# Reordering the first stage of a fused adaLN, linear-attention and GeGLU kernel: an earlier modulation quarter, two loads issued from ACT, and the eighth K tile ahead of the last wk rows

## The chip, the cores and the metric

The kernel runs on one core of a Trainium2 chip. The metric is the device time of one execution in microseconds (us), and a kernel's number is the median of its runs. Engines, as these traces have them: PE does matmuls (PEld is its weight load), DVE and ACT do elementwise work, POOL small things, SP issues DMAs.

## The reference, cut to what matters

```python
mod = (silu(c) @ w_mod).reshape(1, 6, 1, -1)          # w_mod: 1024 x 6144
sa, ca, ga, sb, cb, gb = (mod[:, i] for i in range(6))
h = layernorm(x) * (1 + ca) + sa                      # x: 1 x 2048 x 1024
x = x + ga * linear_attention(h, wqkv, wo)            # 32 heads; divides by pq . z
h = layernorm(x) * (1 + cb) + sb
x = x + gb * ((gelu(h @ w_gate) * (h @ w_up)) @ w_down)   # 3584 wide
```

Linear attention needs K and V of all tokens before any output, and each output is divided by a denominator per token and head. The first K matmul needs tokens, their layer norm, one quarter of the modulation (w_mod is loaded in quarters, because K's contraction goes over 8 rows of weights, two to a quarter) and two rows of wk.

## The kernel before

A helper records each operation in its engine's program, with its semaphores; in the trace PE's instructions start in the order of its program (from 7.03 us: transposes, seven fillers at 7.49, transposes at 9.28, one filler at 9.74, modulation at 9.95, six fillers at 10.76). PE's first stage in the kernel before (V = DVE, A = ACT, Q = SP in the code; `warm` are filler matmuls on zeros, `k_part(q, cs)` the K matmuls of weight rows 2q and 2q+1 for token tiles `cs`, `mod_cols(q)` the matmuls of modulation quarter q, `mod1` applies it on DVE, `t1` transposes on PE). K of the first four token tiles comes in two halves each, which makes eight K tiles. Seven of them are summed up side by side by `k_part`, each in its own bank of PSUM; the eighth, `kv_mm(3, "k", 1, 4, ...)`, has bank 4:

```python
sch.dma(Q, lambda e: e.dma_start(C8[:], c_v), ...)          # c, first of SP's DMAs
...
x_dma(0, 1); x_dma(1, 2); wmq_dma(0, (1,)); x_dma(2, 3)     # all from SP
wmq_dma(0, (0,)); x_dma(3, 4)
...                                                         # wk rows 2q, 2q+1 after quarter q
warm(12, 7)
...
t1(1, 6); warm(1, 7); mod_cols(0, 4, False); warm(6, 7)
...                                                         # tiles 2 and 3, quarters 1 to 3
k_part(2, [3])
warm(2)
k_part(3, [0, 1, 2, 3])                                     # 7 PSUM banks, rows 6 and 7
for (c_, jg), b in kb0.items():
    k_evac(c_, jg, b)                                       # ACT exp, DVE min, DVE add
kv_mm(3, "k", 1, 4, list(range(NDC)))                       # eighth K tile, bank 4
k_evac(3, 1, 4)
for c_ in range(4):
    for jg in range(2):
        b = nb()                                            # V in banks 0, 1, 2, 3 in turn
        kv_mm(c_, "v", jg, b, list(range(NDC)))
        v_evac(c_, jg, b)
```

## Time and profile before

| | before |
|---|---|
| median of the first runs | 847.55 us (845.94 to 847.57, 3 runs) |
| span of the profiled run (which took 846.43 us), mean PE clock | 844.6 us, 1.000 |
| first V matmul | 31.97 us |
| PE waits between 205 and 250 us | 0.89 and 1.26 us |

From PE's timeline of the first stage (start, duration, engine, line, operation, output<-inputs, count; in brackets the idle time before it and what ended that). L519 are transposes, L565 the modulation, L612 K and V, L668 fillers.

```profile
12.05 0.61 PE L519 MATMUL ps_all<-ident,xh 128*128 128x128 bf16 x8
...
19.75 0.54 PE L565 MATMUL ps_all<-siluT,wmq 128*128 128x1 bf16 x16
21.48 0.55 PE L565 MATMUL ps_all<-siluT,wmq 128*128 128x1 bf16 x16 [1.19 <-DMA wmq<-in_w_mod_dram]
...
25.56 0.94 PE L565 MATMUL ps_all<-siluT,wmq 128*128 128x1 bf16 x32
...
26.79 0.59 PE L668 MATMUL ps_all<-warm 128*128 128x512 bf16 x2
27.22 4.91 PE L612 MATMUL ps_all<-wk,h1T 128*128 128x512 bf16 x22
31.97 2.35 PE L612 MATMUL ps_all<-wv,h1T 128*128 128x512 bf16 x10
```

The third transposes start at 12.05, PE waits 1.19 us for a quarter of w_mod at 21.48, and K ends without a break in V at 31.97.

```profile
231.89 2.50 DVE L879 TENSOR_TENSOR pq<-pq,rb 128x512 bf16<-128x512 bf16 x4 [2.35 <-DMA rb<-scr_rd]
...
236.78 2.50 DVE L879 TENSOR_TENSOR pq<-pq,rb 128x512 bf16<-128x512 bf16 x4 [1.25 <-DMA rb<-scr_rd]
```

DVE waits for the broadcasts (2.35 and 1.25 us), PE for DVE (0.89 and 1.26 us). These two waits are the only ones of over 0.7 us between the start of V and the last matmul.

### The profile page before, as it was taken

The page shows a single profiled execution, that of the slowest core. Times are in us where ns is not written, and L with a number is a line of the kernel's source. Part 1 is how long each engine was busy: PE and PEld are TensorE (multiplying, and loading weights), DVE is VectorE, ACT ScalarE, POOL GpSimd, SP SyncE. Part 2 cuts the span into 40 slices and gives each one's busy share as a digit, 9 for nine tenths or more (in the row PEclk, how much of TensorE's full clock was granted, in tenths as well). Part 3 has the DMA queues.
Part 4 walks back from the last instruction along what each step waited for, and adds up shares of the span by engine and source line. Part 5 has one row for each costly group of instructions (what it writes and reads, how often), then busy time and mean ns, then how long its engine had stood idle before and what let it go on. Part 6 is the DMA issues. An engine that isn't in the chain of part 4 may idle for free.

```text
span 844.6 us, 11333 instructions
## 1 busy us (share of the span) xinstructions
PE 835.1 (99%) x4229; PEld 386.9 (46%) x4229; DVE 491.8 (58%) x883; ACT 294.9 (35%) x483; POOL 24.3 (3%) x64
## 2 busy tenths in 40 slices
PE   8999999999989999999999999999999999999998
PEld 4454444444434444444444444444444444444445
DVE  5676767877775555564456665445556635565522
ACT  2343333345504345520344442034544204444300
POOL 2000000000200000010000001000000000000000
PEclk9999999999999999999999999999999999999999
DMA  9991824029957587341455533055553305555000
GB/s 283 355 284 26 262 53 98 14 59 238 197 119 222 157 264 205 100 107 31 126 156 154 156 107 81 26 155 151 150 150 100 75 19 156 151 153 145 7 19 26
DMA packets 181750, 112.70 MB, mean 133 GB/s; under 512 B 33080, under 2 KB 172728, under 8 KB 180672
## 3 DMA queue, kind: packets, MB, share of 16 engines
q1 hardware_dynamic: 181696, 111.98, 48.6%
q8 instruction: 34, 0.56, 0.3%
q14 instruction: 20, 0.16, 0.1%
HBM read 100.67 MB, written 4.47 MB: 124 GB/s over the span
## 4 chain that ended last, share of the span: by engine, by line
PE 92%; DMA 4%; SPq 2%; DVE 1%; issue 0%; ACT 0%; DVEq 0%; ACTq 0%
PE ps_all L1025 23%; PE ps_all L1000 23%; PE ps_all L997 23%; PE ps_all L612 12%; PE ps_all L653 6%; PE ps_all L928 3%; DMA rb<-scr_rd 1%; DMA wmq<-in_w_mod_dram 1%; DMA h2T<-xh 1%; PE ps_all L634 1%; DVE pq L879 1%; DMA scr_rd<-rdc 1%; SPq L443 0%; SPq L438 0%; PE ps_all L584 0%; SPq L868 0%
## 5 line engine op out<-in xcount | busy, mean ns | idle before, releaser
L997 PE MATMUL ps_all<-h2T,wg 128*128 128x512 bf16 x896 | 339.6, 379 | 0.0
L1000 PE MATMUL ps_all<-h2T,wu 128*128 128x512 bf16 x896 | 339.6, 379 | 0.0
L1025 PE MATMUL ps_all<-wd,yT 128*128 128x512 bf16 (+1 forms) x924 | 194.1, 373 | 0.0
L1008 ACT ACTIVATE q<-ps_all 128x512 f32<-128x512 f32 x112 | 66.9, 597 | 233.9 <-PE ps_all L997 233.9
L1025 PEld LDWEIGHTS ps_all<-wd,yT 128*128 128x128 bf16 x924 | 90.4, 98 | 103.3
L1000 PEld LDWEIGHTS ps_all<-h2T,wu 128*128 128x128 bf16 x896 | 87.7, 98 | 105.7
L997 PEld LDWEIGHTS ps_all<-h2T,wg 128*128 128x128 bf16 x896 | 87.7, 98 | 105.7
L1010 DVE SCALAR_TENSOR_TENSOR ww<-q,ps_all 128x512 f32<-128x512 f32 x112 | 77.0, 687 | 92.5 <-ACT guh L1009 92.5
L1013 DVE SCALAR_TENSOR_TENSOR ww<-th,guh 128x512 f32<-128x512 f32 x112 | 77.5, 692 | 77.9 <-ACT th L1012 77.9
L1012 ACT ACTIVATE th<-ww 128x512 f32<-128x512 f32 x112 | 70.5, 629 | 84.3 <-DVE ww L1010 84.3
L1015 DVE TENSOR_TENSOR yT<-ww,ps_all 128x512 bf16<-128x512 f32 x112 | 76.9, 687 | 3.8
L1030 DVE TENSOR_TENSOR ps_all<-ps_all,gbb 128x512 f32<-128x512 f32 (+1 forms) x33 | 22.5, 682 | 94.8 <-PE ps_all L1025 94.8
L1009 ACT ACTIVATE guh<-ps_all 128x512 f32<-128x512 f32 x112 | 66.3, 592 | 0.0
L601 ACT ACTIVATE eb<-ps_all 128x512 f32<-128x512 f32 x64 | 37.5, 601 | 78.5 <-PE ps_all L612 38.8
L653 PE MATMUL ps_all<-h1T,wq 128*128 128x512 bf16 x256 | 58.9, 379 | 0.7 <-DVE pq L604 0.7
L928 PE MATMUL ps_all<-w,pq 128*128 128x512 bf16 x256 | 56.6, 379 | 2.1 <-DVE xall L935 2.1
L612 PE MATMUL ps_all<-wk,h1T 128*128 128x512 bf16 x256 | 58.2, 379 | 0.0
L612 PE MATMUL ps_all<-wv,h1T 128*128 128x512 bf16 x256 | 57.7, 379 | 0.0
L602 DVE TENSOR_SCALAR eb<-eb 128x512 f32<-128x512 f32 x64 | 27.1, 424 | 34.6 <-ACT eb L601 34.2
L928 PEld LDWEIGHTS ps_all<-w,pq 128*128 128x128 bf16 x256 | 24.8, 98 | 32.8 <-DVE xall L935 3.1
L612 PEld LDWEIGHTS ps_all<-wv,h1T 128*128 128x128 bf16 x256 | 24.9, 98 | 29.8 <-DVE eb L602 0.3
L612 PEld LDWEIGHTS ps_all<-wk,h1T 128*128 128x128 bf16 x256 | 24.6, 98 | 29.6 <-DVE h1T L538 1.3
(81 smaller groups left out, 397.6 us busy)
## 6 DMA issues: line engine op xcount, KB each, us to landing
wg<-in_B_w_gate_dram SPq DMA_DIRECT2D x56, 512.0 KB, 3.9
wu<-in_B_w_up_dram SPq DMA_DIRECT2D x56, 512.0 KB, 5.1
wmst<-in_w_mod_dram SPq DMA_DIRECT2D x8, 1024.0 KB, 11.5
rb<-scr_rd SPq DMA_DIRECT2D x32, 256.0 KB, 9.0
wd<-in_B_w_down_dram SPq DMA_DIRECT2D x7, 1024.0 KB, 8.2
wmq<-in_w_mod_dram SPq DMA_DIRECT2D x8, 512.0 KB, 7.6
out_dram<-xall SPq DMA_DIRECT2D x31, 128.0 KB, 1.7
xall<-in_A_x_dram SPq DMA_DIRECT2D x3, 1024.0 KB, 11.7
```

The lines of the kernel that those rows point to most:

```text
L612: o = sch.op(T, lambda e, dc=dc: e.matmul(PS(bank), H1[sg][:, dc, ci * P:(ci + 1) * P], W_[:, dc, jg * 512:(jg + 1) * 512], start=(dc == 0 ...
L653: o = sch.op(T, lambda e, dc=dc: e.matmul(PS(b), WQ[:, dc, qc * P:(qc + 1) * P], H1[sg][:, dc, :], start=(dc == 0), stop=(dc == NDC - 1)), ...
L928: last[half] = sch.op(T, lambda e, g=g, half=half: e.matmul(PS(b0 + half), PQ[sg][:, g, ci * P:(ci + 1) * P], W2[:, g, half * 512:(half + ...
L997: og = sch.op(T, lambda e, dc=dc: e.matmul(PS(bg), WG[slot][:, dc, e_ * P:(e_ + 1) * P], H2[sg][:, dc, :], start=(dc == 0), stop=(dc == ND ...
L1000: ou = sch.op(T, lambda e, dc=dc: e.matmul(PS(bu), WU[slot][:, dc, e_ * P:(e_ + 1) * P], H2[sg][:, dc, :], start=(dc == 0), stop=(dc == ND ...
L1008: sch.op(A, lambda e: e.activation(Q1[j][:, :], PS(bg), ACTF.Square, scale=math.sqrt(GELU_A)), prd=pr(bg), wr=rq, note=f"q1 {fc}")
L1009: ogh = sch.op(A, lambda e: e.activation(GUH[j][:, :], PS(bg), ACTF.Copy, scale=0.5), prd=pr(bg), wr=rg, note=f"gh {fc}")
L1010: sch.op(V, lambda e: e.scalar_tensor_tensor(WW[j][:, :], Q1[j][:, :], 1.0, PS(bg), op0=ALU.add, op1=ALU.mult), rd=rq, prd=pr(bg), wr=rw, ...
L1012: sch.op(A, lambda e: e.activation(TH[j][:, :], WW[j][:, :], ACTF.Tanh, scale=GELU_C), rd=rw, wr=rt, note=f"th {fc}")
L1013: sch.op(V, lambda e: e.scalar_tensor_tensor(WW[j][:, :], TH[j][:, :], 1.0, GUH[j][:, :], op0=ALU.add, op1=ALU.mult), rd=rt + rg, wr=rw, n ...
L1015: sch.op(V, lambda e: e.tensor_tensor(YT[:, fc, :], WW[j][:, :], PS(bu), ALU.mult), rd=rw, prd=pr(bu), wr=r_yt(fc), note=f"yT {fc}")
L1025: o = sch.op(T, lambda e, b=b, fc=fc, c0=c0, c1=c1, n=n: e.matmul(PS(b, 0, n), YT[:, fc, ci * P:(ci + 1) * P], WDT[fc // 4][:, fc % 4, c0:c1],
```

## The change

The intent: apply the first modulation quarter to token tiles 0 and 1 and start K on them before tiles 2 and 3 are transposed; let ACT issue c and the second tokens, so that SP's stream of loads begins earlier (SP took 0.41 us to issue c in the trace before); do six of the eighth K tile's matmuls while the last wk rows are on the way, and use fewer fillers (26 instead of 32). Cut to its core:

```diff
-        sch.dma(Q, lambda e: e.dma_start(C8[:], c_v), ...)
+        sch.dma(A, lambda e: e.dma_start(C8[:], c_v), ...)
         x_dma(0, 1)
-        x_dma(1, 2)
-        wmq_dma(0, (1,))
+        x_dma(1, 2, A)
+        wmq_dma(0, (1, 0))
         x_dma(2, 3)
-        wmq_dma(0, (0,))
+        w_dma(WK, OFF_WK, "wk", 1, 0, D, 0, 2)
         x_dma(3, 4)
...      (last two wk rows and the first half of wv as two DMAs each)
-        warm(7, 7)
         ln1_bn(1, 1)
         ln1_fin(1)
+        warm(4, 7)
+        mod_cols(0, 4, False)
+        xhat_dve(1, *xh_buf(1))
+        mod_copy(0, 4)
+        mod1(0, 1, 0, 2)
+        t1(1, 6)
         ln1_bn(2, 0)
-        xhat_dve(1, *xh_buf(1))
-        t1(1, 6)
-        warm(1, 7)
-        mod_cols(0, 4, False)
-        warm(6, 7)
+        warm(3, 7)
+        k_part(0, [0])
+        mod1(1, 1, 0, 2)
         ln1_bn(2, 1)
         ln1_fin(2)
+        k_part(0, [1])
...      (tiles 2 and 3 in the same manner; warm(5) and warm(2) for warm(3) and warm(1))
-        warm(2)
-        k_part(3, [0, 1, 2, 3])
+        kv_mm(3, "k", 1, 4, list(range(6)))
+        for d in (0, 1):
+            k_part(3, [0, 1, 2, 3], (d,))
+            kv_mm(3, "k", 1, 4, [6 + d])
         for (c_, jg), b in kb0.items():
             k_evac(c_, jg, b)
-        kv_mm(3, "k", 1, 4, list(range(NDC)))
...      (V in the order (0,0) (1,0) (0,1) (1,1), then tiles 2 and 3)
```

More of the change, by code (lines that the diff above doesn't have):

```diff
@@ L426, in bass_adaLN_cond__linear_attn_block__geglu_ffn__prompt_kernel, with x_dma @@
             gop(lambda e, k=k: e.memset(bm32f[32 * k:32 * (k + 1), 8 * k:8 * k + 33 * 7 + 1:33], 1.0), wr=r_sm("bm32"))
-        sch.dma(Q, lambda e: e.dma_start(C8[:], c_v), wr=r_sm("c8"), note="c8")
-        def x_dma(c0, c1):
-            return sch.dma(Q, lambda e: e.dma_start(XALL[:, c0:c1, :], x_v[:, c0:c1, :]), wr=r_xs(c0, c1), note=f"x{c0}")
+        sch.dma(A, lambda e: e.dma_start(C8[:], c_v), wr=r_sm("c8"), note="c8")
+        def x_dma(c0, c1, stream=Q):
+            return sch.dma(stream, lambda e: e.dma_start(XALL[:, c0:c1, :], x_v[:, c0:c1, :]), wr=r_xs(c0, c1), note=f"x{c0}")
         def wm_dma(t, sl):
@@ L449, in bass_adaLN_cond__linear_attn_block__geglu_ffn__prompt_kernel @@
         x_dma(0, 1)
-        x_dma(1, 2)
-        wmq_dma(0, (1,))
+        x_dma(1, 2, A)
+        wmq_dma(0, (1, 0))
         x_dma(2, 3)
-        wmq_dma(0, (0,))
+        w_dma(WK, OFF_WK, "wk", 1, 0, D, 0, 2)
         x_dma(3, 4)
-        w_dma(WK, OFF_WK, "wk", 1, 0, D, 0, 2)
         for q in range(1, 4):
             wmq_dma(q)
-            w_dma(WK, OFF_WK, "wk", 1, 0, D, 2 * q, 2 * q + 2)
-        w_dma(WV, OFF_WV, "wv", 2, 0, 512)
+            for d0, d1 in ((2 * q, 2 * q + 2),) if q < 3 else ((6, 7), (7, 8)):
+                w_dma(WK, OFF_WK, "wk", 1, 0, D, d0, d1)
+        w_dma(WV, OFF_WV, "wv", 2, 0, 512, 0, 4)
+        w_dma(WV, OFF_WV, "wv", 2, 0, 512, 4, 8)
         w_dma(WV, OFF_WV, "wv", 2, 512, 1024)
@@ L683, in bass_adaLN_cond__linear_attn_block__geglu_ffn__prompt_kernel, with k_part @@
         kb0 = {(0, 0): 0, (0, 1): 1, (1, 0): 2, (1, 1): 3, (2, 0): 5, (2, 1): 6, (3, 0): 7}
-        def k_part(q, cs):
-            for dc in (2 * q, 2 * q + 1):
+        def k_part(q, cs, dcs=(0, 1)):
+            for dc in [2 * q + k for k in dcs]:
                 for (c_, jg), b in kb0.items():
@@ L698, in bass_adaLN_cond__linear_attn_block__geglu_ffn__prompt_kernel @@
         t1(0, 5)
-        warm(7, 7)
         ln1_bn(1, 1)
         ln1_fin(1)
-        ln1_bn(2, 0)
-        xhat_dve(1, *xh_buf(1))
-        t1(1, 6)
-        warm(1, 7)
-        mod_cols(0, 4, False)
-        warm(6, 7)
+        warm(4, 7)
[4 more added lines that the diff above has]
+        t1(1, 6)
+        ln1_bn(2, 0)
+        warm(3, 7)
+        k_part(0, [0])
+        mod1(1, 1, 0, 2)
         ln1_bn(2, 1)
         ln1_fin(2)
+        k_part(0, [1])
         ln1_bn(3, 0)
         xhat_dve(2, *xh_buf(2))
-        mod_copy(0, 4)
-        mod1(0, 2, 0, 2)
         t1(2, 7)
+        warm(5)
         ln1_bn(3, 1)
@@ L717, in bass_adaLN_cond__linear_attn_block__geglu_ffn__prompt_kernel @@
         mod1(2, 1, 0, 2)
-        k_part(0, [0, 1])
+        k_part(0, [2])
         xhat_dve(3, *xh_buf(3))
-        k_part(0, [2])
+        mod_cols(1, 4)
         t1(3, 7)
-        mod_cols(1, 4)
         mod1(0, 3, 2, 4)
+        warm(2)
+        k_part(1, [0, 1, 2])
         mod1(3, 1, 0, 4)
-        warm(3)
-        k_part(1, [0, 1, 2])
         mod_cols(2, 4)
@@ L730, in bass_adaLN_cond__linear_attn_block__geglu_ffn__prompt_kernel @@
         k_part(1, [3])
-        warm(1)
         k_part(2, [0, 1, 2])
@@ L735, in bass_adaLN_cond__linear_attn_block__geglu_ffn__prompt_kernel @@
         k_part(2, [3])
-        warm(2)
-        k_part(3, [0, 1, 2, 3])
+        kv_mm(3, "k", 1, 4, list(range(6)))
+        for d in (0, 1):
+            k_part(3, [0, 1, 2, 3], (d,))
+            kv_mm(3, "k", 1, 4, [6 + d])
         for (c_, jg), b in kb0.items():
             k_evac(c_, jg, b)
-        kv_mm(3, "k", 1, 4, list(range(NDC)))
         k_evac(3, 1, 4)
         for c_ in range(4):
-            for jg in range(2):
+            for vc, jg in (((0, 0), (1, 0)), ((0, 1), (1, 1)), ((2, 0), (2, 1)), ((3, 0), (3, 1)))[c_]:
                 b = nb()
-                kv_mm(c_, "v", jg, b, list(range(NDC)))
-                v_evac(c_, jg, b)
+                kv_mm(vc, "v", jg, b, list(range(NDC)))
+                v_evac(vc, jg, b)
             if c_ == 0:
```

## The prediction

> **What bounds the kernel now.** The page gives PE 99% of an 844.6 us span; the chain of waits is 92% PE, 4% DMA, at full clock. From about 32 us on PE is never idle (windows: 10.00 of 10.00 us), so only the first 32 us can change, and only the moment at which the V matmuls start (31.97 us in the timeline) carries to the end. That bounds the change to a few us.
>
> **The first stage.** The chain of waits begins with SP's DMA issues and runs to the landing of a w_mod quarter at 21.43 us. After that it is PE alone: 9.9 us of necessary work (two modulations, 40 K matmuls at 0.216 us) plus 0.7 us of fillers and waits (three warm matmuls, two waits of 0.3 us on modulation), to 31.97.
>
> **What the change removes.**
> - SP issues c and the second tokens in 0.41 us each; both go to ACT. [...] DMA moves 310 to 370 GB/s from 10 us on whatever the order, so I expect all landings about 0.45 us earlier (estimate).
> - Three late fillers and the wait for the last modulation, where six matmuls of the eighth K tile now stand: about 0.7 us of PE.
>
> **What it adds.**
> - ACT issues two DMAs before its 1.28 us table load; the first statistics on DVE hardly move (3.95 to about 3.8 us).
> - DVE becomes the early bound: modulations of tiles 0 and 1 stand ahead of later tiles' statistics. With the trace's durations (statistics 0.69, aggregation and epsilon 0.4, normalise 0.55, PSUM copy 1.02, modulation 0.27 a slice) I get the third transposes at 13.9 us instead of 12.05, PE idle 1.6 us before them, the fourth at 17.6 instead of 15.1, and PE at the third modulation quarter at 21.0 instead of 19.75, just when its data lands (21.43 less 0.45). So the early K matmuls buy nothing that the critical chain keeps.
> - Evacuation: before, the eighth K tile's matmuls (1.7 us) came last and hid the emptying of bank 0 (exp, min, add: 1.85 us after its last matmul). Now bank 0's last matmul comes only 1.5 us before the end of K, and V's first needs bank 0. K ends at about 31.25, V starts at about 31.75: of 0.7 us about 0.4 is given back.
>
> **Total.** V starts about 0.25 us earlier (0 to 1 us plausible). The rest is PE-bound and unchanged; V's new order needs no data earlier than it lands, and DVE's later evacuations still finish before the next transposes need them. 847.55 less 0.25 to 0.6 gives **847.0 us, 845.8 to 848.1** eight times in ten; the three runs before spread over 1.6 us. Faster by over 2%: 0.005; within 2%: 0.985; slower: 0.01.
>
> **What would show it.** Right: V's first matmul at 31.4 to 31.9 us, waiting 0.2 to 0.6 us for DVE's evacuation; PE idle over 1 us near 12 to 14 us behind DVE; landings 0.3 to 0.5 us earlier; the rest as before. Wrong: landings unmoved; PE waiting for a DMA at 20 to 26 us; no wait before V.
>
> **What would make it wrong.** [...] A straggling transfer, as that at 21.43, moves by a us. Or DVE is less late than I count: up to 1 us faster.

The sum: 0.7 us of PE less about 0.4 given back, V about 0.25 us earlier, and 847.55 less 0.25 to 0.6 makes 847.0 us. The 0.45 us of earlier landings is an estimate, as it says; in the trace SP's issue of c took 0.41 us.

## More of the kernel before

The reciprocal denominators of the third and fourth token groups are written to DRAM (`scr_rd`) and loaded back, broadcast, by 16 DMAs (`rb_load(2)`, `rb_load(3)`); DVE scales `pq` with them, and PE's output projection `wo_chunk` waits for DVE:

```python
stream_pair(0, 0)                       # gate and up weights, 1 MB a pair, from SP
stream_pair(0, 1)
for c_ in range(12):
    wo_chunk(c_, 6 if c_ == 0 else 2 * (c_ % 2))
    if c_ == 0:
        den(1, 4)                       # reciprocals -> scr_rd
        rb_load(2)                      # 8 broadcast DMAs of 256 KB
    ...
    if c_ == 1:
        rb_load(3)                      # 8 more
    if c_ in (4, 5, 6, 7):
        pq_scale(2 + (c_ - 4) // 2, c_ % 2)
    if c_ < 4:
        ln2_a(c_, False)                # ends in a transposing DMA, h2T<-xh
    ...
stream_pair(0, 2)
```

From the page of the kernel before: busy time, share of the span and instructions of each engine; a DMA queue with its transfers, MB and share; and the chain that ended last, by engine.

```profile
PE 835.1 (99%) x4229; PEld 386.9 (46%) x4229; DVE 491.8 (58%) x883; ACT 294.9 (35%) x483; POOL 24.3 (3%) x64
...
q8 instruction: 34, 0.56, 0.3%
...
PE 92%; DMA 4%; SPq 2%; DVE 1%; issue 0%; ACT 0%; DVEq 0%; ACTq 0%
```

PE is busy for all but 9.5 us. The line of queue 8 looks harmless: 34 transfers, 0.56 MB in all, which is 16 KB each.

From PE's timeline between 232 and 246 us, and DVE's (L928 is the output projection, L879 the scaling with the broadcasts):

```profile
231.72 2.97 PE L928 MATMUL ps_all<-w,pq 128*128 128x512 bf16 x13
235.58 3.63 PE L928 MATMUL ps_all<-w,pq 128*128 128x512 bf16 x16 [0.89 <-DVE xall L935]
240.46 5.78 PE L928 MATMUL ps_all<-w,pq 128*128 128x512 bf16 x26 [1.26 <-DVE xall L935]
```

## The result, and the profile after

| | before | after |
|---|---|---|
| first measurement, median | 847.56 us (845.94 to 847.92, 4 runs) | 847.91 us (847.74 to 847.99, 4 runs) |
| ratio, 95% interval | | 1.0008, 0.999 to 1.0025 |
| second measurement, five rounds on one chip | 846.44 us (845.88 to 847.05, 9 runs) | 848.27 us (847.23 to 848.43, 5 runs) |
| ratio, 95% interval | | 1.0018, 1.0004 to 1.0032 |
| span of the first profiled run, mean PE clock | 844.6 us, 1.000 | 846.2 us, 0.998 |

A ratio is the mean time of one kernel's fast runs over that of the other's fast runs of the same rounds, so it isn't quite the ratio of the medians. All runs here count as fast ones except where said. The first measurement doesn't separate the kernels; the second does, by 0.18%. The changed kernel is slightly slower.

The page of the changed kernel (the line of queue 8 is the same):

```profile
PE 830.9 (98%) x4144; PEld 386.5 (46%) x4223; DVE 492.3 (58%) x885; ACT 294.8 (35%) x483; POOL 24.4 (3%) x64
...
PE 92%; DVE 3%; DMA 3%; ACT 1%; issue 1%; SPq 0%; POOL 0%; DVEq 0%; ACTq 0%
```

PE's busy time here isn't comparable: some matmul records are missing (4144 for 4229, where the change removes six). The first stage of the changed kernel (lines have moved by one: L520 transposes, L566 modulation, L613 K and V, L669 fillers):

```profile
13.95 0.62 PE L520 MATMUL ps_all<-ident,xh 128*128 128x128 bf16 x8 [1.34 <-DVE xh L495]
...
16.03 1.04 PE L613 MATMUL ps_all<-wk,h1T 128*128 128x512 bf16 x4 [0.39 <-DVE h1T L539]
...
17.71 0.61 PE L520 MATMUL ps_all<-ident,xh 128*128 128x128 bf16 x8
...
21.18 0.94 PE L566 MATMUL ps_all<-siluT,wmq 128*128 128x1 bf16 x32
...
25.43 0.94 PE L566 MATMUL ps_all<-siluT,wmq 128*128 128x1 bf16 x32
26.23 5.34 PE L613 MATMUL ps_all<-wk,h1T 128*128 128x512 bf16 x23
31.94 2.33 PE L613 MATMUL ps_all<-wv,h1T 128*128 128x512 bf16 x10 [0.37 <-DVE pk L605]
```

This is nearly what was predicted: the third transposes at 13.95 (13.9 predicted) after 1.34 us of idle PE, the fourth at 17.71 (17.6), PE at the third modulation quarter at 21.18 (21.0), a wait of 0.37 us for DVE before V (0.4), and V at 31.94 (31.75). V starts 0.03 us earlier than before. Yet the span is 1.6 us longer. Comparing the same PE instruction in the two traces shows where: the changed kernel is 0.05 us ahead from 34 us to 222 us, and 1.54 us behind from 251 us to the end. This holds beyond these two: in all fourteen traces of this document, the time from the first V matmul to the first output projection is 170.35 to 170.64 us, and from the first gate matmul to the end 597.16 to 597.27 us. So two kernels here differ by the start of V and by the stretch between the first output projection and the first gate matmul; nothing else differs by more than 0.4 us in all.

```profile
231.68 2.97 PE L931 MATMUL ps_all<-w,pq 128*128 128x512 bf16 x13
236.86 9.41 PE L931 MATMUL ps_all<-w,pq 128*128 128x512 bf16 x34 [2.22 <-DVE xall L938]
```

```profile
233.17 2.50 DVE L882 TENSOR_TENSOR pq<-pq,rb 128x512 bf16<-128x512 bf16 x4 [2.35 <-DMA rb<-scr_rd]
...
238.08 2.50 DVE L882 TENSOR_TENSOR pq<-pq,rb 128x512 bf16<-128x512 bf16 x4 [1.28 <-DMA rb<-scr_rd]
```

The broadcasts land later: DVE starts the scalings at 233.17 and 238.08 instead of 231.89 and 236.78, both 1.3 us later. PE waits 2.22 us in one piece instead of 0.89 and 1.26. The windows view (busy time of PE, PEld, DVE, ACT, POOL in a stretch, then granted PE clock, DMA share, GB/s) shows a second thing at the same place, first before, then after:

```profile
235.00:240.00 5.00, 3.63 (x16) 1.49 (x16) 3.75 (x6) 0.00 (x0) 0.00 (x0) 1.00 0.99 200
240.00:245.00 5.00, 4.54 (x21) 2.07 (x22) 5.00 (x16) 0.00 (x0) 0.00 (x0) 1.00 0.63 172
```

```profile
235.00:240.00 5.00, 3.14 (x11) 1.23 (x12) 3.72 (x7) 0.00 (x0) 0.00 (x0) 0.80 1.16 230
240.00:245.00 5.00, 5.00 (x21) 2.16 (x20) 4.50 (x10) 0.00 (x0) 0.00 (x0) 0.85 0.84 218
```

The clock is 1.00 in both stretches before, and 0.80 and 0.85 after. The clock records of the changed kernel's trace say that PE ran at half its clock from 238.05 to 241.46 us ("clock halved" below).

### The profile page after: what moved, and what is told of

Read it like the earlier page. It is cut to its first block, busy times and chain, and to the rows that moved or that the text cites. A ratio compares the mean times of both kernels' runs of the same rounds, so it can differ in the third digit from the quotient of the medians.

```text
span 846.2 us, 11248 instructions
## 1 busy us (share of the span) xinstructions
PE 830.9 (98%) x4144; PEld 386.5 (46%) x4223; DVE 492.3 (58%) x885; ACT 294.8 (35%) x483; POOL 24.4 (3%) x64
## 4 chain that ended last, share of the span: by engine, by line
PE 92%; DVE 3%; DMA 3%; ACT 1%; issue 1%; SPq 0%; POOL 0%; DVEq 0%; ACTq 0%
PE ps_all L1003 23%; PE ps_all L1028 23%; PE ps_all L1000 21%; PE ps_all L613 12%; PE ps_all L654 6%; PE ps_all L931 3%; DMA rb<-scr_rd 2%; PE ps_all L635 1%; PE ps_all L669 1%; DVE h1T L539 1%; DVE pq L882 1%; DMA scr_rd<-rdc 1%; PE ps_all L585 0%; PE ps_all L566 0%; PE ps_all L520 0%
## 5 line engine op out<-in xcount | busy, mean ns | idle before, releaser
L1000 PE MATMUL ps_all<-h2T,wg 128*128 128x512 bf16 x859 | 325.6, 379 | 0.0
L613 PE MATMUL ps_all<-wk,h1T 128*128 128x512 bf16 x253 | 57.9, 379 | 0.6 <-DVE h1T L539 0.4
L613 PE MATMUL ps_all<-wv,h1T 128*128 128x512 bf16 x255 | 57.5, 379 | 0.4 <-DVE pk L605 0.4
L654 PE MATMUL ps_all<-h1T,wq 128*128 128x512 bf16 x242 | 56.3, 379 | 1.6 <-DVE pq L605 0.7
L613 PEld LDWEIGHTS ps_all<-wv,h1T 128*128 128x128 bf16 x256 | 24.9, 98 | 30.4 <-DVE pk L605 0.9
L613 PEld LDWEIGHTS ps_all<-wk,h1T 128*128 128x128 bf16 x256 | 24.5, 98 | 30.6 <-DVE h1T L539 2.2
```

The lines of the kernel that those rows point to most:

```text
L613: o = sch.op(T, lambda e, dc=dc: e.matmul(PS(bank), H1[sg][:, dc, ci * P:(ci + 1) * P], W_[:, dc, jg * 512:(jg + 1) * 512], start=(dc == 0 ...
L654: o = sch.op(T, lambda e, dc=dc: e.matmul(PS(b), WQ[:, dc, qc * P:(qc + 1) * P], H1[sg][:, dc, :], start=(dc == 0), stop=(dc == NDC - 1)), ...
L1000: og = sch.op(T, lambda e, dc=dc: e.matmul(PS(bg), WG[slot][:, dc, e_ * P:(e_ + 1) * P], H2[sg][:, dc, :], start=(dc == 0), stop=(dc == ND ...
```

## The experiments

Twelve kernels ran, all correct. They fell on several chips, so each is compared with the runs of the kernel before on its own chip (846.25 to 846.63 us).

### Is the loss there in both kernels by chance?

Two theories at first. *Chance*: the loss at 230 to 250 us comes and goes in either kernel. *Change*: the changed first stage makes it. Both kernels ran again unchanged; and both ran with the wait taken away, by loading what is waited for earlier:

```diff
         stream_pair(0, 0)
-        stream_pair(0, 1)
         for c_ in range(12):
...
+        stream_pair(0, 1)
         stream_pair(0, 2)
```

> The kernel before, unchanged, to see how its own runs differ. Chance theory (the 1.6 us that the traces differ by arise at 230 to 250 us, where PE waits for the broadcast reciprocals, and come and go from run to run in either kernel): runs fall in two groups, near 846 and near 847.6 us, most of them in the upper one, and the upper ones show a mean clock of about 0.998 instead of 1.000. Rival, that the change itself makes the loss by moving the later transfers: nearly all runs here have clock 1.000, and whatever makes 847.6 is something else.

> The changed kernel, unchanged. Chance theory: the same two groups as the kernel before, 846 and 847.6 to 848 us, ratio 0.999 to 1.001. Rival: always near 847.9, with clock below 1.000. In both, V's first matmul at 31.9 us, 0.3 to 0.4 us of it a wait for DVE.

> The kernel before with one line moved: the second pair of gate and up weights (1 MB) is issued after the broadcast loads of the reciprocals instead of before them. Those loads then land about 3 us earlier [...], PE's two waits of 0.9 and 1.3 us at 234 to 240 us go, and with them any halving of the clock. Expected 843.5 to 845 us, all runs at clock 1.000 and within 0.4 us of each other. If the spread of 846 to 847.6 stays, it doesn't come from that wait.

> The changed kernel with the same line moved. With that wait gone the two kernels differ by their first stage alone: chance theory and my reading of the traces (V starts 0.03 to 0.05 us earlier) expect it within 0.2 us of the kernel before with the line moved. Rival, that the change costs about a us later on: 1 us or more slower than it.

| kernel | median, range | ratio to before, 95% | runs with mean clock under 1.000 |
|---|---|---|---|
| before_again | 846.58 (846.24 to 847.17) | 1.0001, 0.9989 to 1.0014 | 0 of 5 |
| after_again | 848.27 (847.23 to 848.43) | 1.0018, 1.0004 to 1.0032 | 1 of 5 |
| before_rb | 845.25 (844.87 to 846.83) | 0.9991, 0.9978 to 1.0003 | 2 of 5 |
| after_rb | 844.22 (843.68 to 845.05) | 0.9974, 0.9961 to 0.9986 | 0 of 5 |

Chance falls: the kernel before stays near 846.5, the changed one near 848.3. The halved clock isn't the main cause either: four of the five runs of after_again had the full clock, at 847.2 to 848.4 us. Its profiled run was one of those:

```profile
237.08 3.63 PE L931 MATMUL ps_all<-w,pq 128*128 128x512 bf16 x16 [2.09 <-DVE xall L938]
241.99 4.27 PE L931 MATMUL ps_all<-w,pq 128*128 128x512 bf16 x18 [1.28 <-DVE xall L938]
```

PE waits 2.09 and 1.28 us, at full clock. The weight load of the first gate matmul of the next stage starts at 248.69 us here and at 248.79 in the first trace, with its half clock: there the half clock took the place of the second wait and cost almost nothing more.

The moved line gave a surprise. It made the changed kernel faster by 4.0 us, but the kernel before by only 1.2 us (medians, same chip), which isn't clear of noise (0.9978 to 1.0003). So now the changed kernel was ahead, by 1.0 us in the medians and by 0.83 us in the stretch of the traces (42.93 for 43.76 us). Both expectations were missed: the two kernels weren't within 0.2 us of each other, and before_rb didn't stay under 845 us, ran over 2 us of range instead of 0.4, and had two runs below the full clock. In the kernel before with the line moved, PE still waits:

```profile
239.22 7.08 PE L928 MATMUL ps_all<-w,pq 128*128 128x512 bf16 x31 [1.06 <-DVE xall L935]
```

In the changed kernel with the line moved, hardly:

```profile
206.47 31.25 PE L931 MATMUL ps_all<-w,pq 128*128 128x512 bf16 x141
237.95 7.08 PE L931 MATMUL ps_all<-w,pq 128*128 128x512 bf16 x31 [0.23 <-DVE xall L938]
```

A cause that hurts the changed kernel in one arrangement and the kernel before in the other can't be a plain cost of the change.

### Is it PE's instruction fetch?

The packet records offer a cause. Queue 8, the harmless line, is of the kind "instruction" and carries 34 transfers of 16 KB, spaced through the span like PE's instructions: the trace of the kernel before counts 8684 for PE and PEld (4229 each, and 226 of their sequencer, which the page leaves out), which is 255 for each transfer, and between the starts of one transfer and the next 170 to 326 of them start, 252 on average. So this is taken to be PE's program being fetched, about 255 instructions at a time; that is the estimate from these counts, as no record names the engine. One such fetch falls among the broadcasts in every trace, and takes 1.0 to 1.6 us. The only other instruction queue, 14, carries transfers of up to 8 KB and has none between 200 and 235 us in any trace. Six fillers fewer are 12 instructions fewer (before_m6 has 4223 of PE and of PEld for 4229), so if the theory holds each later fetch should come that much later in the work: six matmuls at 0.216 us (54 took 11.68 us in the chain of the kernel before), about 1.3 us by estimate. The fetch was at 221.6 and 221.7 us in the two traces of the kernel before, at 224.7 and 225.0 us in those of the changed one. That is 3 us, more than the 1.3; why is open.

*Fetch theory*: when the fetch falls at a bad place among the broadcasts, later ones land about a us later. *Rival*: the DMAs moved to ACT, or the new order of transfers, cause it. Three edits tell them apart. In after_f6 six fillers stand in PE's idle time, so the program is as long as before:

```diff
         k_part(0, [1])
+        warm(6)
```

> The changed kernel with six filler matmuls put where PE waits 1.3 us for DVE (before the third transposes), so that its PE program is as long as before: 32 fillers instead of 26. Fetch theory (the change shortened PE's program by 12 instructions; the 16 KB transfer that fetches PE's instructions then falls at 224.7 instead of 221.6 us, among the last of the first eight broadcast loads, and all later ones land 1.3 us later): the fetch is back near 221.6 us, the last broadcast lands near 236.7 instead of 238 us, and the time is 846 to 847 us, 1 us or more under the changed kernel's 848.2 on this chip. Rival (the transfers moved to ACT, or the new order, do it): still 848 us and the last broadcast near 238 us.

In before_m6 six fillers are taken out of the kernel before, and nothing else:

```diff
-        warm(7, 7)
+        warm(4, 7)
...
-        warm(6, 7)
+        warm(3, 7)
```

> The kernel before with six fillers fewer (four and three instead of seven and six in the first 12 us, where PE waits for data anyway), nothing else. Fetch theory: PE's fetch moves to about 224.7 us, the last broadcast lands near 238 us and the time goes to 847.5 to 848.5 us. Rival: unchanged, 846.4 us, last broadcast near 236.7.

In before_act only the issue of c and the second tokens moves to ACT (the first three edits of the change, without the new order):

> The kernel before with c and the second tokens issued from ACT, nothing else: PE's program is unchanged. Fetch theory: the stretch at 215 to 240 us stays as before, last broadcast near 236.7 us; landings of the first stage some 0.5 to 1 us earlier, V's first matmul 0 to 0.7 us earlier, time 846 to 846.6 us. Rival (the transfers on ACT's queue cost later): 847.5 us or more.

| kernel | median, range | ratio to before, 95% | runs with mean clock under 1.000 |
|---|---|---|---|
| after_f6 | 846.99 (846.33 to 847.07) | 0.9998, 0.9986 to 1.001 | 0 of 5 |
| before_m6 | 848.55 (847.28 to 849.91, 6 runs) | 1.0021, 1.0009 to 1.0033 | 6 of 6 |
| before_act | 846.34 (845.84 to 846.68) | 0.9993, 0.9981 to 1.0005 | 0 of 5 |

The fetch theory's times came in on all three, if before_m6's 848.55 us, just over the expected 848.5, is let pass (its last broadcast landed at 237.2 instead of 238 us). Taking six fillers out of the kernel before, with no other edit, reproduces the whole loss; putting six into the changed kernel removes it; the moved DMAs don't cost anything. PE at the place in question, first after_f6, then before_m6:

```profile
235.71 3.63 PE L932 MATMUL ps_all<-w,pq 128*128 128x512 bf16 x16 [1.20 <-DVE xall L939]
240.60 5.57 PE L932 MATMUL ps_all<-w,pq 128*128 128x512 bf16 x25 [1.27 <-DVE xall L939]
```

```profile
236.09 10.28 PE L928 MATMUL ps_all<-w,pq 128*128 128x512 bf16 x39 [2.14 <-DVE xall L935]
```

after_f6 has the two short waits of the kernel before, before_m6 the long one of the changed kernel.

A smaller dose was tried next, three fillers instead of six:

> The changed kernel with three fillers added instead of six (29 in all). Fetch theory: PE's fetch at 215 to 230 us falls between the two seen so far (220.5 to 221.7 with 32 fillers, 224.2 to 225.0 with 26), near 222 to 224 us; fast (846.3 to 847 us, last broadcast under 20 us after the first) if it falls ahead of the eighth broadcast's data, slow (848 us, over 20 us) if with or after it. Rival (the fillers matter in themselves, not by the fetch): time in the middle, near 847.5 us, with no tie to where the fetch falls.

It ran in 847.97 us (847.76 to 848.17), ratio 1.0016. The fetch was at 225.0 us, not between, so that expectation was missed: three fillers hardly move the fetch, six move it by 3 to 4 us, counted from the first broadcast (in the pair with the moved line, below, by 1.3). But the time again went with the fetch, and there was no middle value.

The strongest test uses the surprise above. If only the place of the fetch among the broadcasts counts, then the edit of before_m6, which cost the kernel before 2 us, must help it once the weights' issue is moved:

> The kernel before with the weights' issue moved (845.25 us, fetch 8.2 us after the first of the second sixteen broadcasts, broadcasts spread over 20.8 us) and with six fillers fewer in the first 12 us. Fetch theory: what counts is where the fetch falls among the broadcasts, not how many fillers there are. With the fillers gone the fetch moves on by 0.5 to 3 us, to 9 us or more after the first broadcast, as in the changed kernel with the weights moved (9.5 us); the spread falls to 19.8 or 19.9 us, and the time FALLS, to 844 to 844.6 us, by the same edit that made the kernel before 2 us slower. Rival (fillers keep PE or its clock in better state, or a shorter program is slower): unchanged or slower, 845.3 to 847 us.

It ran in 844.41 us (844.00 to 845.00), ratio 0.9975 (0.9962 to 0.9989), all runs at full clock: 0.8 us faster than before_rb by the medians, which come from two chips, and lower in the ratio, 0.9975 for 0.9991, though the two intervals overlap. The traces are clearer: the stretch went from 43.76 to 42.64 us, and PE has no wait left where it had 1.06 us:

```profile
229.74 15.38 PE L928 MATMUL ps_all<-w,pq 128*128 128x512 bf16 x68
```

The spread was 19.90 us, the fetch at 9.5 us: all as the fetch theory said, with the sign turned round.

All fourteen traces, sorted by where the fetch of that stretch begins, counted from the landing of the first of the 16 broadcasts; "spread" is from the first broadcast's landing to the last one's:

```
kernel              fetch after first landing   spread     PE idle 205-250
after_f6                   3.4 us              19.68 us      2.47 us
before_act                 3.3                 19.62         2.65
before                     4.7                 19.71         2.15
before_again               4.7                 19.78         2.86
after_again                7.1                 20.29         3.36
after                      7.4                 20.74         2.22, clock halved
before_m6                  7.7                 20.70         2.14, clock halved
after_f3                   7.7                 20.76         2.29, clock halved
before_rb                  8.2                 20.79         1.06
after_rb                   9.5                 19.88         none over 0.3
after_rb_bank              9.5                 19.91         none over 0.3
before_rb_m6               9.5                 19.90         none over 0.3
before_best                9.5                 19.81         none over 0.3
after_rb_bank_act         10.1                 19.87         none over 0.3
```

Five traces with the fetch at 7.1 to 8.2 us have a spread of 20.3 to 20.8 us, the nine others 19.6 to 19.9. In the bad place the fetch meets the last of the first eight broadcasts or the transposing DMA behind them: in the changed kernel the eighth broadcast landed 2.67 us after the seventh (224.40 and 227.07), in before_m6 the transposing DMA 2.45 us after the eighth broadcast (224.80 and 227.25), where 1.0 to 1.2 us is usual. In the good place it also delays a broadcast (222.94 to 225.05 in the kernel before), but the next broadcast and the transposing DMA follow 0.73 and 0.97 us apart and the time is made up.

The traces show one way by which the delay reaches PE. The kernel's helper keeps at most eight DMAs of SP in flight, so the sixteenth broadcast is issued when the DMA eight before it, the transposing one, has landed: within 0.02 us of that in all fourteen traces. From the chain of waits of the kernel before, then of after_again (start, duration, what):

```profile
217.66 9.09 DMA h2T<-xh
226.76 9.89 DMA rb<-scr_rd
```

```profile
218.26 10.01 DMA h2T<-xh
228.28 9.90 DMA rb<-scr_rd
```

The broadcast takes equally long in both; the transposing DMA takes 0.92 us longer in after_again, and all of it is handed on. Counted from the first broadcast's landing, that DMA lands after 9.7 to 9.9 us in the four traces with the earliest fetch, after 10.4 to 10.9 us in the five bad ones, and after 9.3 to 9.4 us in the five with the latest fetch, which begins only when it has landed. It isn't the only way: the twelfth broadcast of the changed kernel was issued 4.8 us after the first one's landing, as before, and landed 1.0 us later all the same.

What is shown: taking six fillers out of PE's program, or putting six in, makes or undoes the loss, and in which direction depends on the arrangement of the loads. That the fetch is the link fits every trace, but no run moved the fetch by itself, without the program. Why the time is made up after an early fetch and not after one at 7 to 8 us stays open.

### What was the first stage worth?

Does V wait for the emptying of bank 0, and was DVE the early bound, as predicted? Both were tried on after_rb, where nothing later hides a gain. First the last two K rows bank by bank instead of row by row, so that bank 0 is finished earlier:

```diff
         kv_mm(3, "k", 1, 4, list(range(6)))
-        for d in (0, 1):
-            k_part(3, [0, 1, 2, 3], (d,))
-            kv_mm(3, "k", 1, 4, [6 + d])
+        for (c_, jg), b in list(kb0.items()) + [((3, 1), 4)]:
+            kv_mm(c_, "k", jg, b, [6, 7])
```

> The changed kernel with the weights' issue moved as before (844.2 us), and the last two K tiles taken bank by bank instead of row by row. If V's wait of 0.3 to 0.4 us is for the emptying of bank 0, as the prediction had it, bank 0 is now done 1.3 us earlier, the wait is gone, and V starts where K ends: 0.35 us earlier than in that kernel, 843.8 to 844 us. If the wait is for something else, it stays.

It ran in 843.93 us (843.28 to 844.16), ratio 0.9963. PE's timeline of after_rb and then of after_rb_bank:

```profile
25.05 0.94 PE L566 MATMUL ps_all<-siluT,wmq 128*128 128x1 bf16 x32
25.86 5.34 PE L613 MATMUL ps_all<-wk,h1T 128*128 128x512 bf16 x23
31.57 2.76 PE L613 MATMUL ps_all<-wv,h1T 128*128 128x512 bf16 x12 [0.37 <-DVE pk L605]
```

```profile
25.72 0.94 PE L566 MATMUL ps_all<-siluT,wmq 128*128 128x1 bf16 x32
26.52 5.34 PE L613 MATMUL ps_all<-wk,h1T 128*128 128x512 bf16 x24
31.70 2.54 PE L613 MATMUL ps_all<-wv,h1T 128*128 128x512 bf16 x11
```

The wait of 0.37 us is gone. From the last modulation matmuls to V it is 6.52 us in after_rb (25.05 to 31.57) and 5.98 us in after_rb_bank (25.72 to 31.70). V's start itself isn't earlier as expected; in this trace the second tokens landed 0.7 us later (6.22 for 5.51 us) and the early stage came later with them.

Then the modulation of tiles 0 and 1 goes from DVE to ACT, which is mostly idle there (busy 1.02 of the 5 us from 9 to 14 us in the trace of after, DVE 4.37):

```diff
-        mod1(0, 1, 0, 2)
+        mod1_act(0, 1, 0, 2)        # the same as an ACT activation with scale and bias
...
-        mod1(1, 1, 0, 2)
+        mod1_act(1, 1, 0, 2)
```

> The kernel of the last run (844 us) with the modulation of the first two K tiles of token tiles 0 and 1 on ACT instead of DVE (four operations of 0.27 us). If DVE is the early bound, as the prediction had it, the third transposes come 0.7 to 1.1 us earlier (13 instead of 14 us), PE reaches the third modulation quarter at 20.0 to 20.5 us, and V starts 0.4 to 1 us earlier than with DVE (31.5 to 31.7): 843.2 to 843.7 us. Rival, that transfers bound the stage: transposes earlier, but V's start unmoved.

```profile
13.28 0.61 PE L520 MATMUL ps_all<-ident,xh 128*128 128x128 bf16 x8
...
20.50 0.94 PE L574 MATMUL ps_all<-siluT,wmq 128*128 128x1 bf16 x32
...
30.73 3.62 PE L621 MATMUL ps_all<-wv,h1T 128*128 128x512 bf16 x16
```

It ran in 843.01 us (842.68 to 843.43), ratio 0.9958. With the second tokens landing at 6.25 us, as in after_rb_bank, the third transposes come at 13.28 instead of 14.23 us, the third modulation quarter at 20.50 instead of 21.46, and V at 30.73 instead of 31.70: 0.97 us earlier. The last two quarters of w_mod landed 0.2 us earlier too, which is far from all of it: DVE was the bound, as far as one pair of traces can show. The runs alone don't separate these steps: the intervals of after_rb (0.9961 to 0.9986), after_rb_bank (0.9951 to 0.9975) and after_rb_bank_act (0.9946 to 0.9971) overlap.

Last, the kernel before keeps its own order of work at the start and takes only the repairs: c and the second tokens from ACT, the weights' issue moved, the eighth K tile in the wait with the last rows bank by bank, V's new order, three late fillers gone.

> The kernel before, with its own order of work at the start, c and the second tokens from ACT, the weights' issue moved, six of the eighth K tile's matmuls in the wait for the last modulation, the last two K tiles bank by bank, V in the new order, and three late fillers gone. Expected: V starts near 31.0 us (31.4 to 32.0 in the kernel before) without a wait, time 843.3 to 844.5 us. If the changed order at the start were worth something in itself, this would be slower than the changed kernel with the same two repairs (843.9 us).

```profile
24.63 0.94 PE L565 MATMUL ps_all<-siluT,wmq 128*128 128x1 bf16 x32
25.43 5.34 PE L612 MATMUL ps_all<-wk,h1T 128*128 128x512 bf16 x23
30.61 3.62 PE L612 MATMUL ps_all<-wv,h1T 128*128 128x512 bf16 x16
```

843.01 us (842.59 to 843.12), ratio 0.9957 (0.9944 to 0.9969): V starts at 30.61 without a wait, and the time is 0.3 us better than the expected range. With the same repairs the changed order at the start gives 843.93 us (ratio 0.9963), or 843.01 with ACT's help. So nothing shows that the early modulation and the early K matmuls are worth anything in themselves; which of the repairs before_best owes most to was not separated. before_best and after_rb_bank_act, at 843.0 us, beat both the kernel before (846.56 us on that chip) and the changed one.

## Why the prediction was right or wrong

- **The time.** 847.91 us lies inside the range of 845.8 to 848.1, but the forecast was a gain of 0.25 to 0.6 us, and there was none: a loss of 0.08% that isn't clear of noise in the first measurement, and of 0.18% that is in the second. That the number lies inside the range is luck: the range stood around 847.55 us, from three runs of which two were high, while 31 of 38 later runs of the kernel before stayed under 847 us.
- **"DVE becomes the early bound": right.** Its times came in within 0.2 us (the idle time was 1.34 us for 1.6), and moving four modulations to ACT brought V 0.97 us forward.
- **"of 0.7 us about 0.4 is given back": right.** The wait for bank 0 was 0.37 us in both traces, and it vanished with the bank order.
- **"all landings about 0.45 us earlier": about right, of little use.** The wk rows of the third quarter landed at 22.78, 22.28 and 22.82 us in three traces with the old transfers (before, before_again, before_rb), and at 21.83, 22.63 and 21.90 in three with the new (after, after_again, after_rb): 0.5 us earlier on average, with 0.8 us of scatter. before_act, which moves the issue alone, has 22.43. The kernel with the issue alone moved isn't clear of the one before in time either (0.9993). DMA moved 320, 344 and 360 GB/s at 10 to 20, 20 to 30 and 30 to 40 us in before, and 317, 339 and 361 in after, so its rate hardly depended on which of the two orders it was.
- **"V starts about 0.25 us earlier": mis-sized, and the term was inside the noise.** V's first matmul was at 31.97, 31.41 and 32.01 us in three traces with the old first stage, and at 31.94, 32.30, 31.57 and 32.07 in four with the new one (after, after_again, after_rb, after_f3; after_f6 has 31.81): no gain.
- **"The rest is PE-bound and unchanged": this step failed.** The busy windows had been read up to 150 us only. At 230 to 245 us PE waits for DVE, which waits for loads, and a transfer that is taken for a fetch of PE's own program falls among those loads. With six fillers fewer it fell in a bad place, which is the likely link, and the loads came later: the broadcasts' spread grew by 0.5 to 1.0 us, and the stretch from the first output projection to the first gate matmul from 45.0 and 45.7 us (before, before_again) to 46.7 and 46.2 us (after, after_again), counted between weight loads. Giving the six fillers back (after_f6) undid it, and taking six from the kernel before (before_m6) reproduced it.
- **The clock: a danger that was named at the wrong place.** The record named the early idle of PE as a danger to its clock. The early idle of 1.34 us left the clock at 1.00. The idle that was followed by half the clock was the later wait of 2.22 us, in after from 238.05 to 241.46 us, which is 3.41 us; so it was after 2.14 us in before_m6 (clock 0.69 and 0.97 in the windows 235 to 240 and 240 to 245 us) and after 2.29 us in after_f3 (mean clock 0.998), and not after 2.09 us in after_again (1.000). What decides between these is not shown.
- **Open.** Three of the first four runs of the kernel before were at 847.5 to 847.9 us; only 2 of its 38 later timed runs exceeded 848 us, with a clock of 0.997 and 0.998, and most lay under 847. No trace exists of those three runs.

## What to carry to other kernels

When a gain is under 0.5%, look for every place where the bound engine still waits, over the whole span, before calling the rest unchanged: here the stretch that hung on DMA landings turned 0.05 us ahead into 1.54 us behind. Taking out six fillers or putting them in shifted the transfer that is taken for the fetch of the program, here by 1.3 to 4 us, and it ran for 1.0 to 1.6 us beside the loads; if an edit's effect has no local cause, restore the instruction count in idle time and measure again. The sturdier repair is to take the wait away, here by issuing 1 MB of weights after the loads that are waited for, which was worth 4.0 us in the changed kernel by one line; the 1.2 us in the kernel before aren't clear of noise.
